# GpSimd's loads of k and v held until the transposed q of the batch is there, in a fused Linformer attention and gated feed-forward kernel

## Chip, cores and metric

One core of a Trainium2 chip runs the kernel. The metric is device time in microseconds (us), the median of a few runs. The engines are TensorE (PE), VectorE (DVE), ScalarE (ACT), GpSimd (POOL) and SyncE (SP); the last two issue DMAs here.

## What is computed

```python
def _attn_ref(q, k, v, E, F):            # q, k, v: 8 batches x 8 heads x 1024 x 64
    k_proj = np.einsum('ks,bhsd->bhkd', E, k)      # E, F: 64 x 1024
    v_proj = np.einsum('ks,bhsd->bhkd', F, v)
    scores = scale * np.matmul(q, k_proj.transpose(0, 1, 3, 2))
    attn = softmax(scores)
    return np.matmul(attn, v_proj)

def _moe_ref(x, w_in, w_out):            # x: 8192 x 512, w_in: 512 x 2048, w_out: 2048 x 512
    h = x @ w_in
    g = h * (1.0 / (1.0 + np.exp(-1.702 * h)))
    return g @ w_out
```

The attention's output, heads side by side, is x of the second function. All inputs and the output are float32; the kernel loads them as bfloat16.

## The kernel before

The 8192 tokens are cut into 16 blocks of 512 tokens; two blocks make a batch. A step has a name and a block: `pj@4` is the projection for block 4. Steps of a whole batch are given at its even block; batch b has the blocks 2b and 2b + 1, and "pair b" below is the pair of blocks of batch b.

Attention of a block: `pj` (L670) projects k and v of the batch by E and F; `kb` copies the projected k out of PSUM (L677), `kd` transposes it by a DMA (L679); `vq` and `vx` copy the projected v. `qd` (in the first batches the halves `qda` and `qdb`) transposes q of the batch by a DMA on SyncE's queue (L239). `sc` makes the scores and `va` multiplies by the projected v (both through `eight`, L249), `ex` takes the exponential on ScalarE (L634). `su` sums the exponentials, `den` copies the sums (L653), `ga` spreads them over partitions by a small DMA (L273), `rc` takes the reciprocal (L657), `sr` sends it to DRAM (L661), `sb` brings it back broadcast as rbc (L665), and `mv` multiplies by it and writes xT (L642). In the first blocks `tk`, `tr`, `tm`, `xt` and `xc` do the last part in another way, without rbc.

The feed-forward part uses Strassen's scheme of seven products: `u0.P1` to `u3.P7` are the products of the first layer (L606), `u.c`, `u.d` and `u.g` their copies, sums and gated activations, `xs` and `gs` the sums of the inputs, `F1` to `F7` the products of the second layer (L503), `Fc`, `Fo`, `Fd` their copies and sums, `st` the stores. Blocks 0 and 1 use plain products (`L`, `Lg`, `O`, `oc`).

The order on every engine is the order of the program; no scheduler changes it. After the program's start come three lists written out by a planner: OPEN (530 steps, up to the first repeated steps), STEPS (127 steps, repeated for blocks 4 to 12; a name with +4 is meant for the block 4 later; the steps of a batch are made at even blocks alone), and TAIL (248 steps). A figure behind a colon is the PSUM bank, a letter behind a slash the engine of a copy. An engine runs ahead of the others as far as its semaphores allow, so the place of a GpSimd or SyncE step in a list sets only its order on that queue and which earlier work it can depend on.

GpSimd's queue has the loads. `ld` at batch b loads k and v of batch b + 1 (L58, 1 MB each as bfloat16), into the single buffers that `pj` of batch b reads; `lq` loads q of batch b + 1 in eight pieces (L70), into the single buffer that `qd` of batch b reads, so it waits for that transpose. Where the batch number b is 2 or more, `lq` is preceded by a copy of one element of rbc into a tile `held` (L691), which keeps GpSimd from issuing q before that rbc is there.

Of the kernel before, what the change touches and what calls it, by code (L numbers as in the profile page):

```python
# [17 lines left out]
def kernel(ctx, tc, q, k, v, E, F,  # L18
# [357 lines left out]
    def ffn2_ops(j):  # L376
# [8 lines left out]
        qda@2 sc.0@1:6,5 ex.0.0@1 ex.0.1@1 wi.4@1 O.0.0@0:7 O.2.0@0:2 sc.1@1:0,1 ex.1.1@1 ex.1.0@1 O.2.1@0  # L385
        tk.0.0@1:6 tk.0.1@1:0 O.1.0@0:4 tr.0.0@1 tk.1.1@1:1 O.1.1@0 tk.1.0@1:3 tr.0.1@1 tm.0.0@1 tm.0.1@1
        O.1.2@0 xt.0@1:6 tk.2.1@1:5 tr.1.1@1 tm.1.1@1 tr.1.0@1 tr.2.1@1 tm.1.0@1 O.2.2@0 xc.0@1/D tk.2.0@1:0
        O.2.3@0 tr.2.0@1 xt.1@1:6 O.0.1@0 tm.2.1@1 O.3.0@0:1 tm.2.0@1 O.0.2@0 tk.3.0@1:3 gt@3 O.0.3@0 O.3.1@0
        oc.0@0/A oc.2@0/D tr.3.0@1 ws.2@1 tk.3.1@1:2 tr.3.1@1 tm.3.0@1 xc.1@1/A tm.3.1@1 wi.5@1/D O.1.3@0
        xt.2@1:0 O.3.2@0 xt.3@1:3 O.3.3@0 gt@6 xc.2@1/A xc.3@1/D L.12@1:5 L.11@1:0 oc.1@0/A L.0@1:3 L.9@1:6  # L390
        Lg.11@1 pj@2:0 oc.3@0/D Lg.0@1 kb@2/A L.10@1:2 L.13@1:4 L.5@1:7 ld@2 Lg.12@1 ws.3@1 vx.1@2 Lg.9@1 kd@2
        L.3@1:5 L.15@1:1 Lg.5@1 L.14@1:7 Lg.3@1 vq.0@2/A Lg.13@1 L.1@1:5 L.2@1:3 Lg.15@1 Lg.14@1 ws.0@1 ws.4@1
        ws.1@1 L.6@1:6 vx.0@2 Lg.1@1 vq.1@2/D ws.5@1/D Lg.2@1 Lg.6@1 Lg.10@1 L.7@1:5 sc.0@2:3,0 sc.1@2:6,7
        Lg.7@1 qdb@2 L.8@1:1 ex.0.0@2 tk.0.0@2:3 ex.1.0@2 tr.0.0@2 ex.0.1@2 tk.0.1@2:5 tm.0.0@2 Lg.8@1 s0.0@0
        s0.1@0 tr.0.1@2 tk.2.1@2:2 tk.1.1@2:3 tk.1.0@2:4 tm.0.1@2 L.4@1:0 tr.1.0@2 tr.1.1@2 Lg.4@1 tm.1.0@2
        tk.2.0@2:4 tm.1.1@2 xt.0@2:5 tr.2.1@2 tr.2.0@2 tm.2.1@2 xt.1@2:3 xc.0@2/D xc.1@2/D gs3.0@1 ex.1.1@2
        pj@4:6 sc.1@3:2,0 sc.0@3:3,1 gs1.0@1 ex.1.0@3 F1.0@1:7 tm.2.0@2 xs.0@2 gs1.1@1 ex.0.0@3 tk.3.1@2:5
        ex.1.1@3 ex.0.1@3 tr.3.1@2 tm.3.1@2 F1.1@1 su@3:0,2 tk.3.0@2:5 Fc1@1:3/A F5.0@1:1 den.0@3/D tr.3.0@2
        den.1@3/A tm.3.0@2 xt.2@2:0 F2.0@1 kb@4/A gs2.1@1 gs2.0@1 xc.2@2/A u1.P1@2:5 xt.3@2:4 F6.1@1 gt@7 gt@5
        u1.c1@2:2/A xc.3@2/D xs.2@2 u1.P5@2:4 F6.0@1 xs.1@2 gs3.1@1 xs.3@2 F5.1@1 u1.P6@2 u1.P2@2 F2.1@1 ga@3  # L400
        u1.c3@2/A Fc3@1/D u0.P1@2:0 Fc2@1/A u1.P3@2 u1.g11@2 F7.1@1 gs4.0@1 gs4.1@1 u1.c2@2/A rc@3 u0.c1@2:5/D
        Fo0@1/D u0.P2@2 u1.d2@2 u0.P6@2 u0.c2@2/D gt@2 u0.g11@2 u0.P5@2:7 u0.c3@2/A F7.0@1 u0.P7@2 vq.0@4/D
        Fd1@1 lq@2 u1.P7@2 kd@4 u1.d1@2 u0.P3@2 u3.P1@2:4 F4.1@1 u1.g12@2 u1.P4@2 sr@3 F4.0@1 vq.1@4/A u0.d2@2
        F3.1@1 u0.d1@2 Fo1@1/D u1.g21@2 u3.c1@2:6/A u0.g12@2 u1.g22@2 u0.g22@2 u0.P4@2 u2.P1@2:0 u3.P6@2
        u3.P5@2:3 gs1.0@2 gs3.0@2 F3.0@1 u0.g21@2 u3.c2@2/A u2.P5@2:7 u2.c1@2:2/D u3.P2@2 u3.P7@2 Fd2@1
        u3.c3@2/A ld@4 u3.P3@2 u2.P6@2 u2.P2@2 u2.c3@2/D u3.d1@2 qd@4 u3.g22@2 u3.P4@2 u2.c2@2/D u2.P3@2 u2.d2@2
        u3.g11@2 u2.P7@2 u2.g11@2 u3.g21@2 sc.1@4:1,4 ex.1.1@4 ex.1.0@4 pj@6:7 gs2.0@2 u3.d2@2 u2.d1@2
        sc.0@4:0,5 u2.P4@2 F1.0@2:4 ex.0.0@4 ex.0.1@4 kb@6/D su@4:1,5 sb@3 F1.1@2 den.0@4/D va.0@3:3,0 u2.g21@2
        Fc1@2:1/A den.1@4/D va.1@3:6,2 u2.g22@2 u3.g12@2 st0@1 st1@1 kd@6 mv.0.1@3 mv.0.0@3 xs.0@3 u2.g12@2
        mv.1.1@3 ga@4 mv.1.0@3 gs1.1@2 vq.1@6/A vq.0@6/A F2.1@2 F2.0@2 Fo0@2/A u1.P1@3:3 u1.P5@3:0 u1.c3@3/D  # L410
        xs.1@3 gs2.1@2 sc.0@5:2,7 ex.0.1@5 sc.1@5:4,5 ex.1.0@5 ex.0.0@5 F5.0@2:6 F5.1@2 gs3.1@2 ex.1.1@5 F6.1@2
        F6.0@2 Fc3@2/A u0.P5@3:2 rc@4 xs.2@3 Fc2@2/A u1.P3@3 u0.P1@3:7 u1.c1@3:4/D gt@1 u1.P2@3 u1.P6@3
        u1.c2@3/A F7.1@2 u0.c1@3:5/A u1.g11@3 xs.3@3 u1.P7@3 u0.c3@3/D F7.0@2 u1.d2@3 u1.d1@3 u0.P2@3 u0.P6@3
        gs4.1@2 u0.P3@3 u1.P4@3 u3.P1@3:3 u0.g11@3 ld@6 Fd1@2 lq@4 u3.c1@3:7/D u0.c2@3/A u1.g12@3 F4.1@2 gs4.0@2
        F4.0@2 u0.d2@3 u3.P6@3 u1.g21@3 su@5:0,2 u2.P1@3:4 u3.P2@3 Fo1@2/D u1.g22@3 den.1@5/D u0.P7@3 u3.c2@3/A
        u2.P5@3:1 u0.d1@3 u2.c1@3:2/A u3.g11@3 den.0@5/A u0.g12@3 sr@4 u0.g22@3 u2.P6@3 F3.1@2 sb@4 u0.P4@3
        u2.c2@3/D u2.c3@3/A u2.P2@3 u3.P5@3:0 gs1.0@3 u3.c3@3/A u2.P7@3 u2.P3@3 F3.0@2 u3.P3@3 u2.d1@3 u2.d2@3
        u3.P7@3 u2.g11@3 u2.g12@3 u2.g22@3 Fd2@2 u3.d2@3 u2.P4@3 F1.0@3:3 va.0@4:4,1 u3.g12@3 u3.d1@3 u3.g22@3
        ga@5 mv.0.0@4 gs1.1@3 qd@6 va.1@4:6,0 mv.1.0@4 u2.g21@3 u0.g21@3 gs2.0@3 st0@2 F1.1@3 mv.0.1@4 u3.P4@3
        rc@5 xs.0@4 u3.g21@3 F5.0@3:4 gs2.1@3 gs4.1@3 Fc1@3:2/A mv.1.1@4 F5.1@3 Fc3@3/A F2.1@3 F2.0@3 gs4.0@3  # L420
        F6.1@3 gs3.1@3 st1@2 gs3.0@3 sc.1@6:7,5 sc.0@6:1,0 F6.0@3 ex.1.0@6 ex.1.1@6 F3.1@3 F3.0@3 Fc2@3/A xs.1@4
        Fo0@3/D ex.0.0@6 u0.P1@4:5 xs.2@4 u1.P1@4:7 F7.1@3 u0.P5@4:1 Fd2@3 u1.c1@4:6/D ex.0.1@6 u1.P2@4
        u0.c1@4:3/D F7.0@3 u1.P6@4 u1.P5@4:0 sr@5 u1.c2@4/A gt@4 xs.3@4 u0.P2@4 u0.P6@4 u3.P1@4:4 u1.c3@4/D
        Fd1@3 u0.g11@4 u0.c3@4/A u1.g11@4 u1.P3@4 F4.0@3 F4.1@3 Fo1@3/A u1.d2@4 u0.c2@4/D su@6:7,5 u3.c1@4:0/D
        den.1@6/A u0.P7@4 u0.P3@4 u2.P1@4:2 den.0@6/A u2.c1@4:7/A u0.d2@4 u1.P7@4 u3.P6@4 u1.g12@4 u2.P6@4 sb@5
        u0.d1@4 u2.P5@4:5 u0.g22@4 u3.c2@4/D u2.c3@4/D u0.g12@4 u2.c2@4/A u2.P2@4 u3.P2@4 u3.P5@4:1 u3.P7@4
        u2.P7@4 u1.d1@4 u1.P4@4 u0.P4@4 u2.d1@4 u1.g22@4 u3.c3@4/A u1.g21@4 u3.g11@4 u3.P3@4 u3.d1@4 u2.P4@4
        u2.P3@4 u3.d2@4 u2.g11@4 u3.P4@4 u2.d2@4 u0.g21@4 va.0@5:4,1 mv.0.1@5 u2.g21@4 u3.g21@4 u2.g22@4
        u3.g12@4 gs1.0@4 va.1@5:2,6 st0@3 lq@6
    """.split()  # L430
    STEPS = """
        F1.0 pj+4 ld+4 mv.1.1+1 u3.g22 mv.0.0+1 u2.g12 mv.1.0+1 xs.0+1 gs2.0 ga+2 sc.1+3 sc.0+3 kb+4 F1.1
        u1.P1+1 vq.0+4 vq.1+4 gs1.1 xs.1+1 gs2.1 Fc1 kd+4 ex.1.1+3 u1.P5+1 F2.1 ex.1.0+3 u1.c3+1 F2.0 Fo0 xs.3+1
# [9 lines left out]
        ga@15 F1.0@13:3 u2.g12@13 u3.g22@13 st1@12 mv.0.0@14 F1.1@13 mv.1.0@14 xs.0@14 mv.1.1@14 Fc1@13:1/D  # L443
        gs1.1@13 u1.P1@14:5 u1.c1@14:7/A xs.1@14 xs.2@14 gs2.1@13 gs2.0@13 gs3.0@13 u1.P5@14:6 u0.P1@14:2
        u0.P5@14:4 u1.P2@14 F2.0@13 u1.P6@14 F5.0@13:0 F6.0@13 F2.1@13 gs3.1@13 gs4.1@13 u1.g11@14 u1.c3@14/D
        Fo0@13/A F5.1@13 u0.c3@14/D rc@15 F6.1@13 Fc3@13/D Fc2@13/D u1.c2@14/D sr@15 gs4.0@13 u0.c1@14:5/A
        u0.P6@14 u1.P3@14 u3.P1@14:3 F7.1@13 F7.0@13 u0.P2@14 u0.P3@14 u1.d2@14 u0.c2@14/D xs.3@14 u0.d2@14
        u1.P7@14 Fd1@13 u0.g11@14 u3.c1@14:4/A u0.g12@14 u1.g12@14 u0.P7@14 F3.0@13 u3.P6@14 u2.P1@14:6 F3.1@13
        sb@15 u0.d1@14 u3.c2@14/D u2.c1@14:2/D Fd2@13 F4.0@13 F4.1@13 u1.d1@14 u3.P2@14 u3.P5@14:0 u2.P6@14
        u2.P2@14 u3.P7@14 u0.P4@14 u0.g22@14 u1.g22@14 u3.c3@14/A u3.g11@14 u2.c2@14/D u0.g21@14 gs1.0@14  # L450
        u3.d1@14 u3.P3@14 u1.P4@14 Fo1@13/D st0@13 u3.d2@14 u2.P5@14:3 u2.g11@14 u1.g21@14 u3.P4@14 u2.c3@14/A
        va.0@15:6,1 va.1@15:7,5 mv.0.0@15 u2.P7@14 mv.1.0@15 u2.d1@14 F1.0@14:0 u2.P3@14 F1.1@14 mv.0.1@15
        u3.g12@14 u2.g22@14 u2.P4@14 xs.0@15 Fc1@14:1/A u2.g21@14 u2.d2@14 mv.1.1@15 u3.g21@14 u0.P1@15:7
        u2.g12@14 u3.g22@14 u1.P1@15:6 u0.c1@15:5/D u1.c1@15:4/A xs.1@15 gs1.1@14 gs2.0@14 u0.P5@15:3 gs2.1@14
        u2.P1@15:2 F2.0@14 u0.c3@15/A u0.P6@15 u1.P2@15 u1.P6@15 F2.1@14 u0.P3@15 xs.2@15 gs3.1@14 Fo0@14/D
        gs3.0@14 u0.c2@15/A xs.3@15 F6.1@14 u0.d2@15 u1.g11@15 F6.0@14 u0.P7@15 u1.P5@15:6 F5.0@14:0 u0.P2@15
# [336 lines left out]
```

## Time and profile before

| | |
|---|---|
| median of 3 runs | 479.17 us (478.61 to 480.8) |
| profiled execution | 478.54 us, its span 476.8 us |
| clock granted to TensorE | 0.995 |
| TensorE busy | 460.2 us (97%) |
| VectorE, ScalarE, GpSimd busy | 344.5, 311.6, 81.2 us |
| DMA | 69.19 MB, mean 145 GB/s |

The span runs from the first to the last instruction. The opening list begins at about 37 us, the first repeated steps at about 168 us, the tail at about 411 us. Times in a timeline are from the span's start. In a row of a timeline, what stands in brackets is how long the engine was idle before, and what ended the wait. An engine's idle time costs something only where it holds up TensorE, which is busy nearly throughout.

### The profile page before, as it was taken

To read this page: it belongs to the slowest core of one execution; us is meant where nothing else is said; L and a number is where in the kernel's file an instruction comes from. 1 tells how busy PE (TensorE), PEld (TensorE's weight loads), DVE (VectorE), ACT (ScalarE), POOL (GpSimd) and SP (SyncE) were. 2 spreads that over 40 slices of the span, in tenths; PEclk is the share of its full clock that TensorE was granted. 3 is DMA by queue.
4 is the path that set the end of the run, shared out by engine and by line. 5 is a ranking of instruction groups with operands and counts; after the bars stand their busy time and mean duration, and the time that the engine had idled before them with its cause. 6 is when DMAs were issued, how large, how long until landed. Compare 5 with 4: busy or idle time off the path is not lost.

```text
span 476.8 us, 10623 instructions
## 1 busy us (share of the span) xinstructions
PE 460.2 (97%) x4378; PEld 362.8 (76%) x4378; DVE 344.5 (72%) x621; ACT 311.6 (65%) x538; POOL 81.2 (17%) x105
## 2 busy tenths in 40 slices
...
GB/s 165 200 188 203 179 180 189 149 198 228 189 142 219 165 94 224 179 114 112 200 205 128 131 114 237 202 96 128 108 135 91 77 92 90 91 91 89 1 44 133
DMA packets 133331, 69.19 MB, mean 145 GB/s; under 512 B 98468, under 2 KB 122532, under 8 KB 133284
## 3 DMA queue, kind: packets, MB, share of 16 engines
q0 software_dynamic: 86496, 29.37, 56.5%
q1 hardware_dynamic: 46708, 38.90, 34.0%
...
## 4 chain that ended last, share of the span: by engine, by line
PE 58%; DMA 16%; issue 5%; DVE 1%; SPq 1%; ACT 1%; POOL 0%; DVEq 0%; POOLq 0%; ACTq 0%
PE k_ps L503 28%; PE k_ps L606 26%; DMA qT<-q_sb 7%; DMA v_sb<-in_v_dram 4%; DMA q_sb<-in_q_dram 2%; DMA rdr<-rc 2%; PE k_ps L249 2%; PE k_ps L670 2%; SPq L665 1%; PE k_ps L648 0%; DVE o_sb L523 0%; DVE sg L374 0%; DMA k_sb<-in_k_dram 0%; ACT L622 0%; POOL v_sb L58 0%
## 5 line engine op out<-in xcount | busy, mean ns | idle before, releaser
L503 PEld LDWEIGHTS <-sg 128*128 128x128 bf16 x960 | 93.6, 98 | 11.9 <-issue 0.8
L606 PEld LDWEIGHTS <-late 128*128 128x128 bf16 x896 | 87.4, 98 | 10.8 <-issue 0.6
L488 DVE TENSOR_TENSOR q_even<-k_ps,q_even 128x512 f32<-128x512 f32 x112 | 74.3, 687 | 26.1 <-PE k_ps L606 23.6
L606 PE MATMUL k_ps<-xw,late 128*128 128x256 bf16 x672 | 90.9, 273 | 0.0
L503 PE MATMUL k_ps<-tw,sg 128*128 128x256 bf16 x720 | 89.4, 273 | 0.0
L622 ACT ACTIVATE gT<-k_ps 128x512 bf16<-128x512 f32 x112 | 63.5, 596 | 36.8 <-PE k_ps L606 27.3
L503 PEld LDWEIGHTS <-gT 128*128 128x128 bf16 x720 | 68.5, 98 | 16.9 <-issue 9.1
L622 ACT ACTIVATE gT<-q_even 128x512 bf16<-128x512 f32 x112 | 65.7, 630 | 23.2 <-DVE q_even L488 20.8
L606 PEld LDWEIGHTS <-w_in_sb 128*128 128x128 bf16 x672 | 65.5, 98 | 9.3 <-issue 1.6
L606 PE MATMUL k_ps<-xT,w_in_sb 128*128 128x256 bf16 x448 | 65.3, 273 | 0.7 <-DVE k_ps L610 0.7
L503 PE MATMUL k_ps<-w_out_sb,gT 128*128 128x256 bf16 x480 | 60.2, 273 | 0.1
L70 POOL DMA_DIRECT2D q_sb<-in_q_dram x56 | 49.0, 905 | 39.2 <-DMA qT<-q_sb 18.2
L374 DVE TENSOR_TENSOR sg<-gT 128x1024 bf16<-128x1024 bf16 x60 | 40.6, 683 | 1.9 <-ACT gT L622 1.9
L634 ACT ACTIVATE expT<-k_ps 128x512 bf16<-128x512 f32 x60 | 32.3, 599 | 8.5 <-PE k_ps L249 8.4
L488 DVE TENSOR_TENSOR o_sb<-k_ps,u_sb 128x512 f32<-128x512 f32 (+1 forms) x31 | 20.8, 669 | 21.7 <-PE k_ps L503 19.4
L642 DVE TENSOR_TENSOR xT<-k_ps,rbc 128x512 bf16<-128x512 f32 x52 | 33.0, 684 | 3.1 <-DMA rbc<-rdr 1.0
L610 ACT COPY k_ps<-k_ps 128x512 f32<-128x512 f32 x37 | 21.2, 573 | 19.0 <-PE k_ps L606 17.8
L606 PE MATMUL k_ps<-xT,late 128*128 128x256 bf16 x224 | 33.4, 273 | 0.0
L523 DVE COPY o_sb<-k_ps 128x512 f32<-128x512 f32 x25 | 17.3, 690 | 20.7 <-PE k_ps L503 17.0
L606 PE MATMUL k_ps<-xw,w_in_sb 128*128 128x256 bf16 x224 | 31.8, 273 | 0.0
L503 PE MATMUL k_ps<-w_out_sb,sg 128*128 128x256 bf16 x240 | 30.6, 273 | 0.0
L503 PE MATMUL k_ps<-tw,gT 128*128 128x256 bf16 x240 | 28.8, 273 | 0.0
...
## 6 DMA issues: line engine op xcount, KB each, us to landing
...
v_sb<-in_v_dram POOLq DMA_DIRECT2D x4, 256.0 KB, 10.7
```

What stands on the lines that cost most here:

```text
L70: nc.gpsimd.dma_start(out=qt[b][:, j], in_=qv[:, j])
L249: nc.tensor.matmul(outs[i][r.start + c:r.start + c + w], lhsTs[i][ri, c:c + w], rhss[i][ri], start=True, stop=True)
L374: nc.vector.tensor_tensor(t[i - 1], in0, in1, op=ALU.add if i == 1 else ALU.subtract)
L488: nc.vector.tensor_tensor(out_, in0, in1, op=ALU.add)
L503: nc.tensor.matmul(dst, x[:, k_, t * P:(t + 1) * P], w[:, k_], start=(first and k_ == 0), stop=(final and k_ == FH - 1), skip_group_check= ...
L523: copy(o(int(i[2]))[:, :, :MH], live["FD" if i == "Fo0" else "FB", j])
L606: nc.tensor.matmul(live[h, j][:, r], a[:, k_, f:f + P], w[:, k_], start=(i in (1, 5) and r == 0 and k_ == 0), stop=(i in (2, 3, 4) and r = ...
L610: copy(new(B_, [P, 2, TH]), live[A, j])
L622: nc.scalar.activation(out_, in_, AF.Gelu_apprx_sigmoid)
L634: nc.scalar.activation(expT[j][:, 2 * n + t, :], live[f"S{n}{t}", j], AF.Exp, scale=scale)
L642: nc.vector.tensor_tensor(x_of(j)[:, n, :], live[f"V{p[1]}{t}", j], rbc[j][:, n, :], op=ALU.mult)
L670: nc.tensor.matmul(kv_ps[r], eft(n, slice(e * KP, (e + 1) * KP)), (kt, vt)[e][b][:, :, n, :], start=(n == 0), stop=(n == J - 1))
```

## The change

Each `ld` is preceded by a copy of one element of the transposed q of the same batch, of its last part, into a second place of the tile `held`. GpSimd runs its queue in order, so k and v of the next batch are not issued before that transpose has landed. In STEPS `ld+4` moves from behind `pj+4` to behind `qd+4`, since a step can wait only for what comes earlier in the program. OPEN and TAIL hold the same steps as before, in an order made anew, with other banks and engines for some. In the new OPEN `lq@2` comes before `ld@2`, and `ld@2`, `ld@4` and `ld@6` come behind the transposes of their batches.

The core of the diff, with the parts of the new OPEN in which the loads, transposes and projections stand:

```diff
-        F1.0 pj+4 ld+4 mv.1.1+1 u3.g22 mv.0.0+1 u2.g12 mv.1.0+1 xs.0+1 gs2.0 ga+2 sc.1+3 sc.0+3 kb+4 F1.1
...
+        F1.0 pj+4 mv.1.1+1 u3.g22 mv.0.0+1 u2.g12 mv.1.0+1 xs.0+1 gs2.0 ga+2 sc.1+3 sc.0+3 kb+4 F1.1 u1.P1+1
...
+        u1.c1+1 gs3.1 F5.0 u0.P5+1 u1.P6+1 F6.1 st1-1 ex.0.0+3 ex.0.1+3 gt+4 rc+2 sr+2 u0.P1+1 sb+2 qd+4 ld+4
...
-    held = consts.tile([1, 1], F32, name="held")
+    held = consts.tile([1, 2, 1], F32, name="held")
...
         elif i == "ld":
+            nc.gpsimd.tensor_copy(held[:, 1], qT[b][:1, J - 1, 0, :1])
             load_kv(k, kt, b + 1, "k_sb")
             load_kv(v, vt, b + 1, "v_sb")
...
         elif i == "lq":
             if b >= 2:
-                nc.gpsimd.tensor_copy(held, rbc[j - 1][:1, 0, :1])
+                nc.gpsimd.tensor_copy(held[:, 0], rbc[j - 1][:1, 0, :1])
             load_q(b + 1)
```

New OPEN, lines around the steps that the prediction speaks of:

```diff
+        Lg.15@1 wi.4@1 sc.1@2:4,6 sc.0@2:7,0 F1.0@1:2 F1.1@1 ex.0.0@2 ex.1.1@2 gs1.0@1 sc.1@3:5,3 ex.1.1@3
+        sc.0@3:7,6 Fc1@1:1/D lq@2 gs1.1@1 ex.0.1@3 F2.0@1 ex.1.0@3 ex.0.0@3 s0.0@0 F2.1@1 su@3:7,5 ex.0.1@2
...
+        rc@3 F3.0@1 xc.2@2/D tm.3.0@2 F3.1@1 F7.0@1 sr@3 u0.P1@2:0 tm.3.1@2 xs.0@2 u1.P5@2:3 u1.P1@2:4 Fd1@1
...
+        gt@7 ld@2 u0.P7@2 qd@4 u1.d1@2 u0.c3@2/D u0.d1@2 u1.g11@2 u1.P4@2 u3.P1@2:0 u1.g21@2 u0.P3@2 pj@4:4
+        u2.P5@2:2 u1.g22@2 u1.g12@2 u0.d2@2 u0.g12@2 u2.c1@2:3/A kb@4/A u3.c1@2:1/D u2.P6@2 u2.c2@2/D u3.P6@2
+        u0.g22@2 u2.P2@2 u3.P5@2:7 u2.c3@2/D vq.1@4/A vq.0@4/D u2.P7@2 u0.P4@2 u3.P2@2 ld@4 u3.c3@2/D u3.c2@2/A
+        u3.P7@2 u2.g11@2 u3.g11@2 u3.P3@2 u2.P3@2 u2.d1@2 sb@3 u2.g22@2 u0.g21@2 kd@4 gs1.0@2 u2.P4@2 u3.d1@2
+        u2.d2@2 va.0@3:4,5 u2.g21@2 gs2.0@2 u3.P4@2 F1.0@2:3 u3.d2@2 F1.1@2 mv.0.1@3 st0@1 mv.0.0@3 va.1@3:5,7
...
+        u0.P2@3 u0.g11@3 pj@6:0 xs.3@3 ga@4 u1.c1@3:5/A kb@6/A u0.P3@3 u0.P6@3 u0.c2@3/D u0.d2@3 F7.1@2 F5.1@2
...
+        u2.c3@3/D u2.P3@3 u2.d2@3 qd@6 u1.g21@3 F3.1@2 sc.1@6:6,4 u3.c3@3/D sc.0@6:5,1 u2.P7@3 F3.0@2 u2.d1@3
```

New TAIL, the part with u1.c1 and u1.P2 of block 15:

```diff
+        Fc1@14:1/D gs1.0@14 gs3.0@14 xs.3@15 u1.P5@15:3 xs.2@15 u1.c1@15:4/D st0@13 u1.c3@15/D u0.P6@15
+        u0.P5@15:2 u0.P2@15 u2.g22@14 u3.g12@14 gs2.0@14 gs1.1@14 u0.c3@15/D st1@13 gs2.1@14 gs3.1@14 F2.0@14
+        F2.1@14 u1.P2@15 u1.P3@15 u1.P6@15 Fo0@14/A F5.0@14:0 F5.1@14 F6.1@14 u0.P3@15 u0.g11@15 F6.0@14
```

More of the change, by code (lines that the diff above doesn't have):

```diff
@@ L384 @@
     OPEN = """
[L385 to L429, printed above, removed]
+        qda@2 sc.0@1:7,6 sc.1@1:5,4 ex.0.1@1 O.3.0@0:0 ex.1.1@1 ex.1.0@1 ex.0.0@1 O.2.0@0:2 O.1.0@0:1 O.3.1@0
@@ new lines @@
+        tk.2.1@1:6 tk.0.1@1:3 tk.1.1@1:4 tk.0.0@1:5 tk.2.0@1:7 gt@4 O.2.1@0 O.3.2@0 tr.0.0@1 tr.0.1@1 tm.0.1@1
+        tm.0.0@1 O.2.2@0 tr.1.1@1 xt.0@1:3 tm.1.1@1 tk.1.0@1:4 O.3.3@0 O.1.1@0 O.2.3@0 tr.2.1@1 tr.1.0@1
+        tm.1.0@1 tm.2.1@1 tr.2.0@1 oc.3@0/A tm.2.0@1 O.1.2@0 xt.2@1:6 xt.1@1:0 tk.3.0@1:5 tk.3.1@1:4 xc.2@1/A
+        ws.1@1 tr.3.1@1 O.0.0@0:7 O.0.1@0 tr.3.0@1 O.0.2@0 tm.3.1@1 xc.0@1/A tm.3.0@1 xt.3@1:3 O.0.3@0 xc.3@1/A
+        xc.1@1/D L.11@1:5 O.1.3@0 L.1@1:4 ws.2@1 ws.0@1 Lg.11@1 oc.2@0/A Lg.1@1 wi.5@1/A oc.0@0/D ws.3@1
@@ new lines @@
+        L.13@1:6 L.3@1:3 L.0@1:7 ws.4@1 pj@2:4 Lg.13@1 vq.0@2/D vx.0@2 Lg.0@1 L.8@1:6 Lg.3@1 kb@2/A oc.1@0/D
+        L.14@1:0 L.2@1:2 L.5@1:5 Lg.8@1 kd@2 L.12@1:1 L.4@1:3 Lg.5@1 Lg.14@1 qdb@2 L.6@1:7 L.7@1:0 Lg.12@1
+        Lg.4@1 s0.1@0 Lg.6@1 L.10@1:1 L.9@1:3 ws.5@1/D vx.1@2 Lg.7@1 vq.1@2/A Lg.10@1 Lg.2@1 L.15@1:5 Lg.9@1
+        Lg.15@1 wi.4@1 sc.1@2:4,6 sc.0@2:7,0 F1.0@1:2 F1.1@1 ex.0.0@2 ex.1.1@2 gs1.0@1 sc.1@3:5,3 ex.1.1@3
+        sc.0@3:7,6 Fc1@1:1/D lq@2 gs1.1@1 ex.0.1@3 F2.0@1 ex.1.0@3 ex.0.0@3 s0.0@0 F2.1@1 su@3:7,5 ex.0.1@2
@@ new lines @@
+        tk.0.0@2:6 gs3.1@1 gs2.1@1 gs2.0@1 den.0@3/A F6.0@1 den.1@3/D tr.0.0@2 ex.1.0@2 tk.1.0@2:7 tk.1.1@2:0
+        tk.0.1@2:3 tm.0.0@2 gs4.1@1 tr.0.1@2 tr.1.0@2 tm.0.1@2 tm.1.0@2 tr.1.1@2 F5.0@1:6 F6.1@1 tk.2.0@2:7
+        tk.2.1@2:4 tm.1.1@2 gs3.0@1 F5.1@1 xt.0@2:3 Fc2@1/A xt.1@2:0 tr.2.1@2 tr.2.0@2 ga@3 Fc3@1/A tm.2.0@2
+        xc.0@2/A F7.1@1 Fo0@1/A gt@6 tm.2.1@2 xc.1@2/A tk.3.0@2:4 gs4.0@1 xt.2@2:7 tk.3.1@2:3 tr.3.0@2 tr.3.1@2
+        rc@3 F3.0@1 xc.2@2/D tm.3.0@2 F3.1@1 F7.0@1 sr@3 u0.P1@2:0 tm.3.1@2 xs.0@2 u1.P5@2:3 u1.P1@2:4 Fd1@1
@@ new lines @@
+        xt.3@2:7 F4.0@1 u0.c1@2:5/D Fd2@1 xc.3@2/A u1.c1@2:2/D u1.c3@2/A xs.1@2 F4.1@1 u0.P2@2 u1.P6@2 xs.3@2
+        u1.P3@2 u0.P6@2 u1.P2@2 u2.P1@2:6 Fo1@1/D u1.c2@2/D xs.2@2 u1.P7@2 u0.P5@2:1 u0.c2@2/A u0.g11@2 u1.d2@2
+        gt@7 ld@2 u0.P7@2 qd@4 u1.d1@2 u0.c3@2/D u0.d1@2 u1.g11@2 u1.P4@2 u3.P1@2:0 u1.g21@2 u0.P3@2 pj@4:4
+        u2.P5@2:2 u1.g22@2 u1.g12@2 u0.d2@2 u0.g12@2 u2.c1@2:3/A kb@4/A u3.c1@2:1/D u2.P6@2 u2.c2@2/D u3.P6@2
+        u0.g22@2 u2.P2@2 u3.P5@2:7 u2.c3@2/D vq.1@4/A vq.0@4/D u2.P7@2 u0.P4@2 u3.P2@2 ld@4 u3.c3@2/D u3.c2@2/A
@@ new lines @@
+        u3.P7@2 u2.g11@2 u3.g11@2 u3.P3@2 u2.P3@2 u2.d1@2 sb@3 u2.g22@2 u0.g21@2 kd@4 gs1.0@2 u2.P4@2 u3.d1@2
+        u2.d2@2 va.0@3:4,5 u2.g21@2 gs2.0@2 u3.P4@2 F1.0@2:3 u3.d2@2 F1.1@2 mv.0.1@3 st0@1 mv.0.0@3 va.1@3:5,7
+        u3.g22@2 u2.g12@2 u3.g21@2 u3.g12@2 sc.0@4:4,6 gs1.1@2 Fc1@2:1/A sc.1@4:0,2 F2.0@2 F2.1@2 ex.1.0@4
+        ex.1.1@4 ex.0.1@4 xs.0@3 ex.0.0@4 mv.1.1@3 gs2.1@2 F6.0@2 gs4.0@2 Fo0@2/A F6.1@2 st1@1 gs3.0@2
+        sc.1@5:6,2 ex.1.1@5 mv.1.0@3 sc.0@5:0,7 su@4:3,4 u0.P1@3:5 xs.1@3 Fc2@2/D den.1@4/A ex.0.1@5 den.0@4/D
@@ new lines @@
+        F5.0@2:2 ex.1.0@5 xs.2@3 u1.P5@3:3 u0.P5@3:7 u0.c1@3:6/D u1.P1@3:4 gs3.1@2 u0.c3@3/D ex.0.0@5 gs4.1@2
+        u0.P2@3 u0.g11@3 pj@6:0 xs.3@3 ga@4 u1.c1@3:5/A kb@6/A u0.P3@3 u0.P6@3 u0.c2@3/D u0.d2@3 F7.1@2 F5.1@2
+        vq.0@6/A vq.1@6/A u1.P2@3 rc@4 u1.c3@3/A u1.g11@3 su@5:0,7 u0.P7@3 F7.0@2 u0.d1@3 den.1@5/D u1.P6@3
+        u1.P3@3 u0.P4@3 u1.c2@3/A u3.P1@3:7 Fc3@2/D den.0@5/A gt@1 lq@4 u0.g12@3 u2.P1@3:4 Fd1@2 F4.0@2
+        u3.c1@3:0/D u3.P6@3 u3.P2@3 u1.d2@3 u1.P7@3 kd@6 F4.1@2 u1.g12@3 u2.c1@3:3/D u0.g21@3 u3.g11@3 u0.g22@3
@@ new lines @@
+        u1.d1@3 u1.g22@3 sr@4 u2.P6@3 u2.P5@3:6 u3.c2@3/A u1.P4@3 u2.P2@3 u3.P5@3:7 u2.c2@3/A Fo1@2/D u2.g11@3
+        u2.c3@3/D u2.P3@3 u2.d2@3 qd@6 u1.g21@3 F3.1@2 sc.1@6:6,4 u3.c3@3/D sc.0@6:5,1 u2.P7@3 F3.0@2 u2.d1@3
+        gs1.0@3 ex.1.1@6 u3.P3@3 u2.P4@3 u3.P7@3 sb@4 ga@5 Fd2@2 u3.d1@3 ex.0.1@6 F1.0@3:4 st0@2 gs2.0@3 u3.d2@3
+        ex.0.0@6 ex.1.0@6 F1.1@3 u3.P4@3 Fc1@3:1/D va.0@4:6,7 mv.0.1@4 u2.g21@3 va.1@4:5,3 u3.g21@3 F2.1@3
+        F2.0@3 mv.0.0@4 st1@2 mv.1.0@4 u2.g22@3 u2.g12@3 u3.g12@3 xs.0@4 u0.P1@4:7 mv.1.1@4 u3.g22@3 u1.P1@4:0
@@ new lines @@
+        u0.c1@4:5/A u1.P5@4:6 gs1.1@3 xs.1@4 Fo0@3/A gs2.1@3 u0.P2@4 gs4.1@3 u1.c1@4:2/A gs3.0@3 xs.3@4 u0.g11@4
+        F5.0@3:3 xs.2@4 u1.P2@4 rc@5 u1.c3@4/A gt@5 F6.0@3 F6.1@3 u0.P5@4:7 u1.P6@4 u0.P6@4 u1.P3@4 Fc2@3/D
+        F5.1@3 u1.c2@4/D u0.c3@4/A sr@5 u0.c2@4/A u0.P3@4 u1.g11@4 gt@2 u3.P1@4:4 gs3.1@3 u0.P7@4 F7.1@3 F7.0@3
+        u0.d2@4 u1.d2@4 u0.d1@4 gs4.0@3 u0.P4@4 Fc3@3/A Fd1@3 gt@3 u1.P7@4 su@6:6,7 F4.0@3 den.1@6/A u3.P5@4:7
+        u1.d1@4 u3.c1@4:0/A u3.P2@4 u0.g21@4 den.0@6/A F4.1@3 Fo1@3/D u1.g12@4 u2.P1@4:5 F3.1@3 u3.g11@4
@@ L430 @@
+        u2.c1@4:4/D u3.P6@4 u2.P5@4:1 u1.g22@4 u0.g22@4 u2.c3@4/D u3.c3@4/A u0.g12@4 u2.P6@4 u2.P2@4 u3.P3@4
+        u3.c2@4/A u2.c2@4/D u2.g11@4 u2.P3@4 u3.P7@4 u3.d2@4 u2.P7@4 u3.d1@4 u1.P4@4 ld@6 F3.0@3 u1.g21@4
+        u2.d1@4 u3.g12@4 u2.g22@4 sb@5 Fd2@3 gs1.0@4 u2.P4@4 u3.P4@4 va.0@5:7,5 u2.d2@4 va.1@5:6,2 mv.0.1@5
+        st0@3 lq@6 u2.g21@4 u3.g21@4
     """.split()
     STEPS = """
-        F1.0 pj+4 ld+4 mv.1.1+1 u3.g22 mv.0.0+1 u2.g12 mv.1.0+1 xs.0+1 gs2.0 ga+2 sc.1+3 sc.0+3 kb+4 F1.1
@@ L433 @@
-        u1.P1+1 vq.0+4 vq.1+4 gs1.1 xs.1+1 gs2.1 Fc1 kd+4 ex.1.1+3 u1.P5+1 F2.1 ex.1.0+3 u1.c3+1 F2.0 Fo0 xs.3+1
-        F6.0 u1.c1+1 gs3.1 F5.0 u0.P5+1 u1.P6+1 F6.1 st1-1 ex.0.0+3 ex.0.1+3 gt+4 rc+2 sr+2 u0.P1+1 sb+2 qd+4
+        F1.0 pj+4 mv.1.1+1 u3.g22 mv.0.0+1 u2.g12 mv.1.0+1 xs.0+1 gs2.0 ga+2 sc.1+3 sc.0+3 kb+4 F1.1 u1.P1+1
+        vq.0+4 vq.1+4 gs1.1 xs.1+1 gs2.1 Fc1 kd+4 ex.1.1+3 u1.P5+1 F2.1 ex.1.0+3 u1.c3+1 F2.0 Fo0 xs.3+1 F6.0
+        u1.c1+1 gs3.1 F5.0 u0.P5+1 u1.P6+1 F6.1 st1-1 ex.0.0+3 ex.0.1+3 gt+4 rc+2 sr+2 u0.P1+1 sb+2 qd+4 ld+4
@@ L442 @@
     TAIL = """
[L443 to L456, printed above, removed]
-        u1.c3@15/A st1@13 u2.c1@15:3/A u1.P3@15 u2.P2@15 u0.d1@15 u0.P4@15 u0.g11@15 u1.c2@15/A u0.g12@15
```

29 lines of the change are left out of this document (21 added, 8 removed).

## The prediction

> **What bounds the kernel now.** I read the page first, then TensorE's waits, then the timelines of TensorE, SyncE and GpSimd at the places where TensorE stops.
>
> ```profile
> PE 460.2 (97%) x4378; PEld 362.8 (76%) x4378; DVE 344.5 (72%) x621; ACT 311.6 (65%) x538; POOL 81.2 (17%) x105
> q0 software_dynamic: 86496, 29.37, 56.5%
> q1 hardware_dynamic: 46708, 38.90, 34.0%
> ```
>
> TensorE is the bound, and the change leaves its set of instructions as it is and only reorders it; so 476.8 - 460.2 = 16.6 us of idle time, and some time at a lower clock, can be won. q0 carries GpSimd's loads of q, k, v, q1 carries SyncE's transposes, stores and small transfers.
>
> TensorE's waits, longest first in total (us, times, longest):
>
> ```profile
> PE k_ps L249 <- DMA qT<-q_sb: 6.6, 5, 3.1
> PE k_ps L563 <- ACT expT L634: 1.7, 2, 1.2
> ...
> PE k_ps L670 <- DMA v_sb<-in_v_dram: 0.8, 1, 0.8
> PE k_ps L606 <- DVE k_ps L610: 0.7, 1, 0.7
> ```
>
> The largest is the scores (L249) waiting for transposed q. The timeline of TensorE says where (start, length, work, idle before it):
>
> ```profile
> 71.06 0.34 PE L563 MATMUL k_ps<-vx,expT 128*128 128x130 bf16 x3 [1.19 <-ACT expT L634]
> 76.64 0.38 PE L670 MATMUL k_ps<-v_sb,eft 128*64 128x512 bf16 x1 [0.79 <-DMA v_sb<-in_v_dram]
> 108.00 0.41 PE L249 MATMUL k_ps<-qT,kt 64*32 64x512 bf16 x8 [3.11 <-DMA qT<-q_sb]
> 147.66 0.41 PE L249 MATMUL k_ps<-qT,kt 64*32 64x512 bf16 x8 [1.50 <-DMA qT<-q_sb]
> 251.09 0.41 PE L249 MATMUL k_ps<-qT,kt 64*32 64x512 bf16 x8 [0.71 <-DMA qT<-q_sb]
> 305.84 0.41 PE L249 MATMUL k_ps<-qT,kt 64*32 64x512 bf16 x8 [0.85 <-DMA qT<-q_sb]
> ```
>
> Most lies in the opening list (about 37 to 168 us), little in the repeated steps, nearly none in the tail. The stage 70 to 79 us also runs at a clock of 0.81:
>
> ```profile
> 70.00:79.00 9.00, 6.27 (x44) 3.25 (x44) 5.92 (x18) 6.33 (x9) 0.00 (x0) 0.81 1.18 187
> ```
>
> Why qT is late: SyncE's queue (length is the issue), and GpSimd's:
>
> ```profile
> 64.09 7.66 SPq L239 DMA_TRANSPOSE qT<-q_sb  x1
> 92.86 12.82 SPq L239 DMA_TRANSPOSE qT<-q_sb  x1
> 140.78 4.87 SPq L239 DMA_TRANSPOSE qT<-q_sb  x1
> 238.31 9.17 SPq L239 DMA_TRANSPOSE qT<-q_sb  x1
> ```
>
> ```profile
> 59.90 0.88 POOL L58 DMA_DIRECT2D k_sb<-in_k_dram  x1 [8.91 <-PE k_ps L670]
> 79.84 7.00 POOL L70 DMA_DIRECT2D q_sb<-in_q_dram  x8 [18.19 <-DMA qT<-q_sb]
> 86.76 0.95 POOL L58 DMA_DIRECT2D k_sb<-in_k_dram  x1
> 87.63 0.96 POOL L58 DMA_DIRECT2D v_sb<-in_v_dram  x1
> 110.55 0.88 POOL L58 DMA_DIRECT2D k_sb<-in_k_dram  x1 [21.96 <-PE k_ps L670]
> ```
>
> With no k or v under way the transpose at 140.78 issues in 4.87 us and lands after 6.74 (147.52). Beside the load issued at 86.76 it issues in 12.82 and lands after 15.1 (108.0), 3 us after v (105.0). The half of a pair at 64.09 lands at 78.9, 2.3 us after v (76.6). So a transpose hardly moves until k and v are in.
>
> **The change part by part.** Sums are against the profiled execution, 478.54 us (span 476.8 and 1.7 around it), which is 0.63 under the median of 479.17.
>
> Lost time is counted from start to start of neighbouring matmuls, beyond their streaming (107 ns for 256 columns); this adds some 0.15 us of restart to each idle time. Opening: 0.63 at 41 us, 4.9 in 70 to 79 (waits for exponentials 2.1, v 1.2, qT 0.6, half-speed clock 1.0), 3.27 at 108, 0.7 around 116, 0.84 at 123.5, 1.66 at 147.7: 12.0. Repeated steps: 0.87 at 251 and 1.02 at 306: 1.9. Tail: 0.2.
>
> *The hold.* Seven one-element copies on GpSimd; the row of the present hold is 0.17 us each, 1.2 in all, off the path. Behind each stand two load issues (0.88 each), the hold on rbc and eight q issues (7.0). Who waits for those: the next projection for k and v, the next transpose for q.
>
> *Repeated steps.* The step ld moves behind the steps rc, sr, sb and qd in the list; none of these is GpSimd's, so on its queue ld still stands just before lq, and SyncE's queue is not reordered. At 224.7 the loads now start at once, k lands at 236.4, v at 242.7, qT at 251.0. Held, qT issues about 237 and lands about 244 (6.74), against a need at 250.1: 6 us to spare, so both stalls go, -1.9. k and v then go from 244.5 and land about 262 (18 us, the slow case), against a projection at 277: 15 us of cover. If that cover were gone, each us late would be a us of TensorE. lq is no later: its own hold on rbc ends at 264.3 in any case.
>
> Here a rule weighs. The row says 15.1 us beside loads and 6.74 alone. The Trainium skill, DMA: Bandwidth & Descriptors, section SWDGE vs HWDGE vs iDMA, says that each DMA engine takes turns between the queues that the two kinds of issuer feed. By turns a transpose would keep half and land after 13.5, and holding the loads would only trade: the same bytes, each set ending later by what the other gains, plus a start-up. By the rule, the transpose at 238.31 would land at about 251, so the gain there stays, but in the opening, where the loads are needed soon, it would be nearly nothing, a total of about -2. By the rows, loads are hardly slowed by a transpose (k and v took 12.3 us from the last q landing with one, 10.5 streaming without), so one side loses little. I take the rows, with caution for the landing: k to v landing took 15.8 to 18.2 us from issue.
>
> *The opening, new order.* Same 530 steps, 116.6 us of matmul streaming by the rows (eight 256-column matmuls 0.87, a projection 1.75), so I place steps by streamed time after 37.1 us and ask what must have landed.
> - qdb issues at 64.1 as now (its q lands at 64.04), now alone: qT of pair 1 at 71. Need: 72. The 0.6 goes.
> - Exponentials: the old list lets ScalarE fall 6.5 us behind and VectorE 6.3 there (summing their rows against streamed time), the new one 3.4 and 3.3. Eight exponentials (0.6 each) behind a table load (1.28) still hold back the row sums and token products that read them: I charge 0.9, where 2.1 and 1.0 of clock were lost.
> - rc of block 3 waits on a small transfer on VectorE's own queue. Behind it xT copies, then x differences, which u1.P5 needs. The bounds are 0 (at 89.71 rc found it landed) and 2.7 (at 122.21 it came 7.9 us after its issue): 0.5, since only q loads are beside it.
> - lq of pair 2 moves ahead of ld and starts at 71 instead of 79.84; its last piece lands about 82 (10.7 after start, row of 156.5). k and v follow from 78, landing near 94.5; the projection now stands at 54.1 of streaming, about 93.5: 1.0 (0 to 3).
> - qT of pair 2 issues about 84.5, beside k and v, landing about 98.5. Need: 103. The 3.27 goes.
> - After it SyncE issues rbc (sb) and the kt transpose: kt lands 6.5 to 7.4 us after issue at 97.5, and scores need it at 103.8; rbc lands 5.3 to 6.3 after 95, or 9 to 11 under loads, and va.1 needs the multiply behind it at 103.5. The two overlap: 1.5 (0 to 4).
> - The held loads of pair 3 go at 99, land at 115 to 117; the projection stands at 113 to 114: 1.5 (0 to 4).
> - q of pair 3 lands near 120, its transpose is alone and lands at 128.3; need 130. The 1.66 goes.
> - The start (41 us) stays, 0.6; small waits on copies, of which the old list has 1.5, 0.7.
>
> Sum: 0.6 + 0.9 + 0.5 + 1.0 + 1.5 + 1.5 + 0.7 = 6.7 against 12.0, -5.3.
>
> *The tail, new order.* 61.7 us of streaming, 0.2 lost today. In the new list VectorE has 11.2 us of work in 5 us of streaming and a backlog of up to 7.7 (4.1 before), with u1.c1 of block 15 in it, on which u1.P2 waits. Between 0 and 1.7: 0.5 charged. The last stores are alike.
>
> Together -1.9 - 5.3 + 0.5 = -6.7: 471.8 for an execution like the profiled one, 472.5 as a median.
>
> **The rivals.**
> 1. *Every transfer fits* (0.15). For it: three of my charges (1.0, 1.5, 1.5) are inside the uncertainty of landing times. Without these and the tail's, 4.5 more: about 468.
> 2. *Waits only move* (0.18). As the rule has it, k and v are late by what qT gains; or the list's ScalarE and VectorE waits equal the old ones. Charges at 3, 4, 4 are 7 more than mine, so nearly nothing is left: about 479.5. That the hold changes nothing, because the projection already ends after qT, belongs here; against it stand 224.7 and 238.3, where the load goes first.
> 3. *Slower: the ring of holds* (0.15). qT lands, then k and v go, then the projection, then kb, the kt transpose (about 8 us) and scores: four links in line where loads ran ahead before. Place: the projections of pairs 2 and 3 at about 93 and 113 us. If qT of pair 2 starves again until 3 us after v and itself issues late, at 90, it lands near 104, v of pair 3 at 121 and its projection waits 8; with 3 at the former projection and 4 at kt that is 15 where I have 4.0, +11, so 483. It decides for slower than today once these three waits pass 10.7 together; by over 0.5% from 13. Against it: 20 us lie between pair 2's hold and that projection.
>
> **How the numbers follow.** My forecast has 0.52, between 469 and 475. About 0.5% (2.4 us) is what this measurement can tell from no change. Faster: 0.52 + 0.15 + 0.03 of rival 2 = 0.70. Same: 0.14 of rival 2. Slower: 0.15 + 0.01. The range takes in both ends of the landing charges and part of rival 3: 467 to 480.5.
>
> **What would show it.** Right: the waits of L249 for qT fall from 6.6 to under 1.5; transposes issue in about 5 us in the repeated steps, with k and v issued after them; pairs of blocks from 222 and 277 us shrink from 54.6 and 54.8 to 53.8; repeated steps begin about 5 us earlier than 167.7; the stage of 0.81 clock is shorter. Wrong: L670 waits for v by over 3 us, L249 for kt, or VectorE for rbc or rc by several us; an opening of over 130 us; a tail with TensorE waiting for VectorE by over 2 us.

## The result and the profile after

The changed kernel takes 471.84 us (median of 4, 471.61 to 473.04) against 479.17: ratio 0.985, interval 0.982 to 0.988. On the chips of two later groups of runs it stood at 0.989 (0.985 to 0.993) and 0.987 (0.984 to 0.990). The profiled execution took 471.61 us, its span is 469.8. A few executions of other runs took far longer than the rest of their kernel (559.7 us and more); the ratios leave them out.

The page, and TensorE's waits:

```profile
PE 458.6 (98%) x4378; PEld 362.8 (77%) x4378; DVE 342.5 (73%) x617; ACT 312.7 (67%) x541; POOL 82.5 (18%) x111
...
q0 software_dynamic: 86496, 29.37, 55.7%
q1 hardware_dynamic: 46708, 38.90, 33.7%
```

```profile
PE k_ps L671 <- DMA v_sb<-in_v_dram: 3.9, 1, 3.9
...
PE k_ps L607 <- ACT k_ps L611: 0.7, 1, 0.7
```

The same matmuls and the same bytes; TensorE's idle time fell from 16.6 to 11.2 us. No score waits for qT any more (6.6 us before). One large wait is left, a projection that waits for v. It stands at 115 us in TensorE's timeline, and the stages show a lower clock there, not at 70 to 79 us as before (last columns: granted clock, DMA share, GB/s):

```profile
115.03 0.59 PE L671 MATMUL k_ps<-v_sb,eft 128*64 128x512 bf16 x1 [3.90 <-DMA v_sb<-in_v_dram]
```

```profile
70.00:79.00 9.00, 8.91 (x98) 6.77 (x96) 6.96 (x19) 6.56 (x11) 7.81 (x10) 1.00 1.89 137
105.00:119.00 14.00, 10.10 (x90) 6.42 (x89) 6.47 (x12) 7.21 (x13) 1.95 (x3) 0.88 1.69 186
```

SyncE's queue, then GpSimd's:

```profile
64.16 2.00 SPq L239 DMA_TRANSPOSE qT<-q_sb  x1
...
82.36 10.63 SPq L239 DMA_TRANSPOSE qT<-q_sb  x1
...
122.20 5.38 SPq L239 DMA_TRANSPOSE qT<-q_sb  x1
...
230.29 7.70 SPq L239 DMA_TRANSPOSE qT<-q_sb  x1
```

```profile
68.99 6.99 POOL L70 DMA_DIRECT2D q_sb<-in_q_dram  x8 [17.89 <-DMA qT<-q_sb]
...
96.91 0.17 POOL L674 CAST held<-qT 1x1 f32<-1x1 bf16 x1 [19.09 <-DMA qT<-q_sb]
98.08 0.88 POOL L58 DMA_DIRECT2D k_sb<-in_k_dram  x1 [1.01 <-PE k_ps L607]
98.95 0.89 POOL L58 DMA_DIRECT2D v_sb<-in_v_dram  x1
...
240.18 0.17 POOL L674 CAST held<-qT 1x1 f32<-1x1 bf16 x1 [22.91 <-DMA qT<-q_sb]
240.69 0.88 POOL L58 DMA_DIRECT2D k_sb<-in_k_dram  x1 [0.34 <-PE k_ps L607]
```

Three of the four transposes shown now have no k or v beside them. The half at 64.16 issues in 2.0 us instead of 7.7, so q of batch 2 starts at 69.0 instead of 79.8. The one at 82.36 still has k and v of batch 2 beside it and still issues in over 10 us; it lands at 96.8, where the scores come at 102.6. In the repeated steps the issue took 7.7 us where 4.9 was the undisturbed row. The broadcast loads of rbc stand just in front of it on SyncE's queue (228.72). They are the probable reason: in the kernel before, the last transpose stands behind rbc too and took 8.7 us without k or v beside it. It comes in time all the same: its hold ends at 240.2, the scores come some 5 us later.

The starts of the projections date the stages. The first of the repeated steps is at 163.9 us (168.6 before), the one of batch 7 at 325.5 (331.8), the last matmul at 466.2 (472.6), the end of the span at 469.8 (476.8). So the opening gave 4.75 us, the repeated steps 1.6, the tail's matmuls nothing, and what follows the start of the last matmul 0.6.

Other transfers changed their speed too. The DMA issues of before, then of after (last column: median us to landing):

```profile
out_dram<-o_sb SPq DMA_DIRECT2D x31, 512.0 KB, 2.8
...
rdr<-rc SPq DMA_DIRECT2D x13, 16.0 KB, 4.9
...
kt<-k_b SPq DMA_TRANSPOSE x7, 7.2
```

```profile
out_dram<-o_sb SPq DMA_DIRECT2D x31, 512.0 KB, 5.9
...
rdr<-rc SPq DMA_DIRECT2D x13, 16.0 KB, 1.4
...
kt<-k_b SPq DMA_TRANSPOSE x7, 3.3
```

The medians are over the issues whose landing the trace tells, which is not all of them. In the repeated steps the transposed k and the reciprocals have no held load beside them any more; the stores have.

### The profile page after: what moved, and what is told of

It reads as the page before. It is cut to its first block, busy times and chain, and to the rows that moved or that the text cites. A ratio compares the mean times of both kernels' runs of the same rounds, so it can differ in the third digit from the quotient of the medians.

```text
span 469.8 us, 10622 instructions
## 1 busy us (share of the span) xinstructions
PE 458.6 (98%) x4378; PEld 362.8 (77%) x4378; DVE 342.5 (73%) x617; ACT 312.7 (67%) x541; POOL 82.5 (18%) x111
## 4 chain that ended last, share of the span: by engine, by line
PE 84%; DMA 11%; ACT 2%; POOL 1%; issue 1%; DVE 1%; POOLq 0%; ACTq 0%
PE k_ps L504 36%; PE k_ps L607 33%; DMA v_sb<-in_v_dram 6%; DMA qT<-q_sb 3%; PE k_ps L547 3%; PE k_ps L315 3%; PE k_ps L671 3%; PE k_ps L249 3%; PE k_ps L553 2%; DMA out_dram<-o_sb 1%; POOL k_sb L58 1%; PE k_ps L649 1%; ACT gT L556 1%; POOL v_sb L58 0%; PE k_ps L564 0%
## 5 line engine op out<-in xcount | busy, mean ns | idle before, releaser
L607 PE MATMUL k_ps<-xw,late 128*128 128x256 bf16 x672 | 89.9, 273 | 0.0
L504 PE MATMUL k_ps<-w_out_sb,gT 128*128 128x256 bf16 x480 | 59.1, 273 | 0.0
L524 DVE COPY o_sb<-k_ps 128x512 f32<-128x512 f32 x22 | 15.2, 692 | 21.9 <-PE k_ps L504 20.0
## 6 DMA issues: line engine op xcount, KB each, us to landing
w_out_sb<-in_moe_w_out_dram POOLq DMA_DIRECT2D x4, 512.0 KB, 11.5
```

The lines of the kernel that those rows point to most:

```text
L504: nc.tensor.matmul(dst, x[:, k_, t * P:(t + 1) * P], w[:, k_], start=(first and k_ == 0), stop=(final and k_ == FH - 1), skip_group_check= ...
L524: copy(o(int(i[2]))[:, :, :MH], live["FD" if i == "Fo0" else "FB", j])
L607: nc.tensor.matmul(live[h, j][:, r], a[:, k_, f:f + P], w[:, k_], start=(i in (1, 5) and r == 0 and k_ == 0), stop=(i in (2, 3, 4) and r = ...
```

## The experiments

Each kernel was run beside the kernel before. That one read 478.5 to 479.3 us from group to group, so ratios are compared. The kernel without holds and the one with the later projection were run twice; lines and waits are those of the second run.

**Hold or order: the new lists without the hold.**

```diff
         elif i == "ld":
-            nc.gpsimd.tensor_copy(held[:, 1], qT[b][:1, J - 1, 0, :1])
             load_kv(k, kt, b + 1, "k_sb")
```

> The new lists as they are, with the hold's copy taken out of ld at every batch; k and v are then issued as soon as the projection has read their buffers and GpSimd reaches them. Theory H (the hold carries the gain): transposes run beside the loads again, the waits of the scores for qT come back in the repeated steps (1.5 to 2 us) and at the scores of blocks 6 (over 5 us, since k and v of batch 4 then go at about 118, in front of the transpose at 122): 477 to 480 us. Theory O (the new order carries the opening, the hold only the steps): k and v of batch 3 go 4 us earlier, which takes away the 3.9 us wait for v at 115 us and its half-speed clock (5.5 us together), and nearly pays for what comes back: 470 to 475 us.

Measured: 481.65 us, 1.007 (1.004 to 1.010): slower than the kernel before, by more than either theory allowed.

> The same kernel as the one with the new lists and no hold, run again for its trace, since the first execution with a profile ran at a clock of 0.80. It took 481.7 us, some 10 us more than the changed kernel. Theory H1 (qT is late in the opening): L249 waits for qT of batch 3, issued at about 122 us behind the loads of batch 4, for 8 us or more, and the repeated steps lose some 2. Theory H2 (several places): qT of batches 2 and 3, the transposed k and the repeated steps lose 2 to 4 us each.

Measured: 481.02 us, 1.005 (1.002 to 1.009). TensorE's waits, the place of the longest, and SyncE's and GpSimd's queues before it:

```profile
PE k_ps L249 <- DMA qT<-q_sb: 8.1, 2, 7.2
PE k_ps L671 <- DMA v_sb<-in_v_dram: 2.9, 1, 2.9
```

```profile
138.84 1.06 PE L249 MATMUL k_ps<-qT,kt 64*32 64x512 bf16 x16 [7.17 <-DMA qT<-q_sb]
```

```profile
123.22 13.47 SPq L239 DMA_TRANSPOSE qT<-q_sb  x1
```

```profile
118.13 0.88 POOL L58 DMA_DIRECT2D k_sb<-in_k_dram  x1 [0.87 <-PE k_ps L671]
119.00 0.88 POOL L58 DMA_DIRECT2D v_sb<-in_v_dram  x1
```

Without the hold k and v of batch 4 leave 4 us ahead of the transpose of batch 3, whose issue takes 13.47 us instead of 5.38. It lands just under 138.8 (the scores start at 138.84), under 3 us after v (136.0). From start to start that wait costs 7.3 us, and 1.28 and 1.12 stand at the scores of two later batches in the repeated steps (at 254 and 309 us; the profile puts the first down to ScalarE, but there too the transpose took 10.4 us to issue): 9.7 together, less the somewhat shorter wait for v. The changed kernel beside it was 8.4 us faster. So the gain is the hold's, in the place that H1 names; the new order without it is a loss. Theory O falls, and its hope for the wait for v too: that fell only to 2.9 us.

**The hold in the repeated steps alone, the opening and tail lists of before.**

```diff
         elif i == "ld":
+            if j >= 8:
+                nc.gpsimd.tensor_copy(held[:, 1], qT[b][:1, J - 1, 0, :1])
...
```

This is against the kernel before; STEPS is that of the changed kernel.

> The opening and tail lists of before, without hold; the hold and the moved ld in the repeated steps alone. Both theories: the two stalls at 251 and 306 us (0.87 and 1.02 us from start to start) go, nothing else moves: 477.3 us, 0.4% under before. If a held load collides with rbc or the q loads in the steps, 479 or more.

Measured: 477.16 us against 478.52, 0.998 (0.996 to 1.000). The interval reaches no change, so the trace has to tell. Of the waits at 251 and 306 us none is left in its trace, but a new one stands at 203 us:

```profile
PE k_ps L606 <- DVE o_sb L523: 0.7, 1, 0.7
```

```profile
202.36 0.69 DVE L523 COPY o_sb<-k_ps 128x512 f32<-128x512 f32 x1 [1.64 <-DMA out_dram<-o_sb]
```

That matmul waits for VectorE's copy of a result, and the copy waits for the store of its buffer. This store, issued at 193.1 us beside the held k and v, took 9.1 us to land. Some of the 1.9 us is given back so: in this trace the repeated steps, from the projection of batch 4 to that of batch 7, are 0.8 us shorter than before.

**The new opening alone, and the tail of before.** The first kernel has the new OPEN with its three holds, and STEPS and TAIL of before; the second is the changed kernel with TAIL of before.

> The new opening list with its three holds; repeated steps and tail as before, without hold. The two late transposes of the repeated steps come back (1.28 and 1.12 us from start to start in the kernel without holds), the opening keeps its gain: 2 to 2.5 us over the changed kernel, 474 to 475.5. If opening and steps are worth the same apart as together, its gain to before and that of the steps alone (1 to 1.4 us) add up to the whole.

> The changed kernel with the tail list of before. The profile of the changed kernel shows one wait in the tail (0.23 us from start to start), as before. If the tails are alike: within 0.5 us of the changed kernel (472 to 473 here). If the new tail's VectorE backlog costs what was charged, 0.5 to 1.7 us less.

> The changed kernel once more beside these, so that differences of one per cent and less are read on one chip: ratio 0.985 to 0.989 to the kernel before.

Measured: 475.33 us, 0.991 (0.988 to 0.994), for the opening alone; 473.59, 0.988 (0.983 to 0.992), with the old tail; 473.20, 0.987 (0.984 to 0.990), for the changed kernel. The whole kernels with the old and the new tail cannot be told apart. The traces show one small difference: from the start of the last matmul to the end it is 3.6 us with the new tail and 4.15 with the old one. Opening and steps add within their intervals: 0.991 times 0.998 is 0.989.

**The old opening with the hold put in.** Each ld of the old OPEN is set behind the transpose of its batch, nothing else is moved; the tail is that of before.

```diff
-        Lg.7@1 qdb@2 L.8@1:1 ...
+        Lg.7@1 qdb@2 ld@2 L.8@1:1 ...
...
-        ... qd@4 u3.g22@2 ...
+        ... qd@4 ld@4 u3.g22@2 ...
...
-        ... qd@6 va.1@4:6,0 ...
+        ... qd@6 ld@6 va.1@4:6,0 ...
```

The lines are shortened, and those from which the three ld are taken are left out.

> The opening list of before, with ld merely moved behind the transpose of its batch and held; the rest as in the changed kernel but with the tail of before. The projection of batch 2 stands 3 us of streaming behind the hold of batch 1's transposes there, and the projection of batch 3 1.6 us behind that of batch 2, so TensorE waits for v some 14 to 18 us at each: 500 to 515 us. If the hold alone does the good and the order little, 472 to 476 us.

Measured: 495.42 us, 1.036 (1.031 to 1.041). Less than expected, but in the places named:

```profile
PE k_ps L670 <- DMA k_sb<-in_k_dram: 11.5, 2, 7.1
PE k_ps L670 <- DMA v_sb<-in_v_dram: 9.0, 2, 4.6
```

Two projections wait 20.5 us for k and v, at 79 and 122 us. So the hold needs the new order as much as the order needs the hold: the projection must stand where its held load can have landed. I had expected 14 to 18 at each and got 8.9 and 11.5. The holds ended at 68.9 and 107.2 us, and v landed 14.1 and 17.8 us after its own issue.

**The wait for v that is left: the load earlier, or the projection later.** First the hold of batch 2 alone is taken out:

```diff
         elif i == "ld":
-            nc.gpsimd.tensor_copy(held[:, 1], qT[b][:1, J - 1, 0, :1])
+            if j != 4:
+                nc.gpsimd.tensor_copy(held[:, 1], qT[b][:1, J - 1, 0, :1])
```

> The changed kernel without the hold at ld of batch 2 alone (it loads k and v of batch 3). If the hold is what makes v late there, k and v go at about 94 instead of 98.1 us, v lands at about 111, and the 3.9 us wait at 115 us and the half-speed projection behind it (1.5 us) go; the transpose issued at 82.4 us is nearly done by then and lands by 99, where the scores need it at 102.6: 466 to 468 us. If the transpose still starves beside these loads, it lands after 103 and one wait replaces the other: 470 to 473 us.

Measured: 472.30 us, 0.986 (0.983 to 0.989), a ratio that cannot be told from the changed kernel's.

```profile
PE k_ps L671 <- DMA v_sb<-in_v_dram: 2.5, 1, 2.5
...
PE k_ps L249 <- DMA kt<-k_b: 1.3, 1, 1.3
PE k_ps L607 <- DVE o_sb L524: 1.1, 1, 1.1
```

GpSimd issues k 3.5 us earlier (94.54), but v comes only 0.3 us earlier (the projection goes on at 114.75), and the transposed k, issued at 94.63, holds up the scores until 103.8. The load itself took longer, 20.2 us from the issue of k to the landing of v instead of 16.9: it now shares the DMA engines with the end of the transpose (landed at 96.8), with rbc and with kt. The wait was exchanged, with kt in the part that I had given to qT.

Second, the projection is set later, in front of su of block 5 and its bank:

```diff
-        u0.P2@3 u0.g11@3 pj@6:0 xs.3@3 ga@4 u1.c1@3:5/A kb@6/A u0.P3@3 u0.P6@3 u0.c2@3/D u0.d2@3 F7.1@2 F5.1@2
-        vq.0@6/A vq.1@6/A u1.P2@3 rc@4 u1.c3@3/A u1.g11@3 su@5:0,7 u0.P7@3 F7.0@2 u0.d1@3 den.1@5/D u1.P6@3
+        u0.P2@3 u0.g11@3 xs.3@3 ga@4 u1.c1@3:5/A u0.P3@3 u0.P6@3 u0.c2@3/D u0.d2@3 F7.1@2 F5.1@2
+        u1.P2@3 rc@4 u1.c3@3/A u1.g11@3 pj@6:0 kb@6/A vq.0@6/A vq.1@6/A u0.P7@3 F7.0@2 u0.d1@3 su@5:0,7 den.1@5/D u1.P6@3
```

> The changed kernel with the projection of batch 3, its copies kb and vq, and su of block 5 set 3.1 us of matmul streaming later in the opening list; holds as in the changed kernel. If the 3.9 us wait for v is a wait of one place, it falls to about 0.8 us, and the half-speed clock behind it goes too: 467 to 469 us. If the wait only moves on (to scores of block 6, whose transposed k comes later), 471 to 473 us.

> The kernel with the projection of batch 3 set 3.1 us later, run again for its trace and beside the changed kernel. Its first ratio was 0.982 against 0.985. If the wait for v was cut as meant, 1 us or less of it is left, and the whole gain should be near 4 us; with 1.3 us seen, the trace should show a new wait of 2 to 3 us at the scores of block 6 or at a copy that stands behind the moved projection.

> The changed kernel as it is, on the chip of the runs beside it: ratio 0.985 to the kernel before, about 471.5 us.

Measured: 470.26 us, 0.982 (0.980 to 0.985), and again 469.80, 0.983 (0.980 to 0.986), where the changed kernel beside it stood at 472.62, 0.989 (0.985 to 0.993). The first is between what the two cases expected. Its waits, and ScalarE's timeline at the first of them:

```profile
PE k_ps L607 <- ACT k_ps L611: 1.5, 1, 1.5
...
PE k_ps L249 <- DMA qT<-q_sb: 1.4, 1, 1.4
PE k_ps L607 <- DVE q_even L615: 0.5, 1, 0.5
```

```profile
140.01 0.59 ACT L524 COPY o_sb<-k_ps 128x512 f32<-128x512 f32 x1 [2.01 <-DMA out_dram<-o_sb]
```

The wait for v is gone, and the granted clock of the whole run is 1.0. Some 1.6 us come back at the scores of block 6: q of batch 3 lands when it did, the transpose is issued at 122.11 as before, and TensorE is there sooner. Another 0.8 us more than in the changed kernel comes back behind a copy that waits on ScalarE for a store, which runs beside the k and v issued at 129.4 us. This version beats both kernels, the changed one by 2.8 us of the group in which both ran. Moves against these two waits were not tried.

## Why the prediction was right, point by point

- *Total.* 471.8 us was worked out for an execution like the profiled one, which took 471.6; the span fell by 7.0 us. The closeness is partly luck, as the terms show. Of the signs named for being wrong one came, a projection waiting for v by over 3 us.
- *Repeated steps, -1.9.* Measured -1.6 by the projections' starts, with k and v landed at 259.0 where the projection comes at 271.6. Right; the kernel with the steps alone gave 1.4, not clear of noise. Two sizes were off against each other: the held transpose took 9.9 us until the hold ended (230.3 to 240.2), not 6.74, but it was issued 12.5 us after the start of the projection, not 14.5, probably because the reciprocals' transfer lands sooner. I had named no cost for the stores that the held loads now stand beside, and the holds are six copies, not seven.
- *Opening, -5.3.* Measured -4.75, but with other parts. The term that was mis-sized most is the charge of 1.5 for the projection of batch 3: it cost 4.1 us from start to start, and some 1.6 more as its matmuls went on at half speed (3.45 us from the first v to the next matmul, 1.84 in batch 2). k and v went at 98.1 and v landed at 115.0, as placed (99, 115 to 117); wrong was when TensorE would be there, 110.7 instead of 113 to 114, because most of the charges ahead of it did not come.
- *The other charges.* The start, 0.6: gone. Exponentials 0.9: some 0.4 seen. rc 0.5: no wait of TensorE. The projection of batch 2, 1.0: none, v landed at 92.0, 2.5 us earlier than I put it. kt and rbc 1.5: 0.2. Small waits on copies 0.7: 0.9, behind the projection. With the 5.7 above that is 7.2 where 6.7 was charged. I had priced kt by its rows of before, 6.5 to 7.4 us, which were themselves rows beside loads; it took a median of 3.3. The same holds for the transfer of the reciprocals, 1.4 us instead of 4.9. A duration that is measured in contention cannot price a kernel that takes the contention away.
- *Tail, +0.5.* None: no wait beyond the 0.2 us that was there. Instead the 0.6 behind the last matmul was won, which I had put at nothing.
- *The rule of taking turns* (the Trainium skill, DMA: Bandwidth & Descriptors, section SWDGE vs HWDGE vs iDMA). The page speaks of turns; that a transpose would then keep half was my own estimate. The rows are slower than this estimate: 14.4 us from issue to landing in the changed kernel and 15.5 in the kernel without holds, beside k and v, where it gives 13.5. An estimate from the landings, with 6.74 us for the whole transpose alone, puts its progress while v was still under way at a fifth to a third of that. But the loads are not free of it: in the kernel before, v lands 6.1 to 7.5 us after k with a transpose of q beside it, and 5.2 in the one case without (123.4 and 128.6 us); in the changed kernel's held loads, with no transpose of q beside them, it is 4.6 to 6.6. This points to a trade, an unequal one. Nor does the 7.3 us decide against the rule, as by halves too the transpose at 123.2 would have been some 5 us late for scores that were ready at 131.5. I was wrong that by the rule a hold gains next to nothing in the opening: the k and v held there have time, landing at 148.4 for a projection at 163.9.
- *The rivals.* The ring of holds exists: it is what the old opening with the hold ran into, 20.5 us in two places. In the new order only one of its links, the projection of batch 3, was short, by 4.1 us of the 10.7 from which it decides.
